# The fourth group's P of each two-layer step transposed by DMA, with a refitted planner and a new order of work

## The chip, the cores and the metric

One core of a Trainium2 chip runs the kernel. The metric is the time of one execution on the device in microseconds, the median of several runs. Beside it stands a profile of one execution, with every instruction's start and end.

The engines go by the profile's names: PE (TensorE: matmuls; PEld is its weight load), DVE (VectorE), ACT (ScalarE), POOL (GpSimd) and SP (SyncE, whose queue issues most of the DMAs). Each engine works through its own instructions in order and waits on semaphores for the others.

## The reference

Two layers, each of attention with a recurrent memory and of a gated feed-forward network, run over x of 2048 rows by 576:

```python
for s in range(n_seg):                      # 64 segments of 32 rows
    h = concatenate([mem, xs], axis=1)      # 8 rows of memory + 32 rows
    q, k, v = (einsum('btd,dhe->bhte', h, W) for W in (Wq, Wk, Wv))   # 32 heads of 128
    scores = where(mask, einsum('bhqe,bhke->bhqk', q, k) * scale, -1e9)
    o = einsum('bhqk,bhke->bhqe', softmax(scores), v)
    o = einsum('bhte,hed->btd', o, Wo)
    mem = o[:, :M, :]                       # the next segment's memory
    outs.append(o[:, M:, :])

x = x + A(layernorm(x), ...); x = x + B(layernorm(x), ...)            # layer 0
x = x + A(layernorm(x), ...); x = x + B(layernorm(x), ...)            # layer 1
# B: silu(x @ w1) * (x @ w3) @ w2, with 4608 hidden columns
```

A segment can't begin before the one ahead of it has given its memory. Both layers use the same weights.

## The kernel before, in words

**Steps.** Attention goes in 72 steps of one segment. Layer 1 runs 8 steps (`LAG`) behind layer 0, so 56 of the steps (8 to 63) work on a segment of each layer at once: 80 columns (2 x 40 rows) instead of 40. The other 16 have one layer. The weights of the attention stay in SBUF; those of the feed-forward network are streamed from HBM again for each 128 rows, into two buffers (W13) for w1 and w3 and two (W2C) for w2.

**Inside a step.** The 32 heads go in four groups of 8. A group takes these nodes, with the letter that each has in the written-out order of PE: Q and q (projections of q and k, 64-row remainder in q, two each per group), S (scores), then on DVE and ACT the softmax (`sm_add`, `sm_max`, `sm_exp`, `sm_sum`, and `sm_pb`, which writes P into the tile PB), then a transpose of P from PB into PTS, then P (P times V), a copy of its result, and O and o (times Wo). V comes from V, v, X, x or G, g. When the fourth o is done, the memory's columns are copied into HT, on which the next step's Q waits. The feed-forward network fills PE beside this: F and f (up), W and w (down), and p, n, a, b are small transposes around the layernorms.

**The transpose of P.** With `g < DMA_GROUPS` in a step with two layers, one DMA on SP's queue does it (`ptd`, L1027): it reads 112 partitions of PB and writes PTS. Otherwise it is the letter T: 8 matmuls with the identity (`ptr`, L1034) into two banks of PSUM, and two copies to PTS on ACT or DVE (`pt_ev`, L1044). PB has one buffer, PTS has two. With `DMA_GROUPS = 3` the fourth group of each such step, and all groups of steps with one layer, use T.

**The planner.** `make_nodes` (L232) makes the nodes with their durations in us, dependences and buffers. `plan` (L77) lays them out in planned time: PE takes its nodes in the order of the string `ORDER` (L222, made of `FIRST`, eleven times `FOUR`, and `LAST`; one `FOUR` is four steps with 18 pairs of the feed-forward network). Each other engine takes the node that can start first in planned time; a copy marked `AD` goes to ACT or DVE, whichever is free first. `LATS` (L33) are planned delays from one engine to the next, `SWITCH` what PE is charged for a new tiling mode; a node marked `full/col` takes the mode of its neighbours, and in `col` each of its matmuls is issued as two halves. `TRD, TRL` (L36) are the planned time of a transpose on SP's queue and its delay after that. The plan decides only the order in each engine's stream and which engine does a copy. When an instruction really starts, semaphores decide.

**SP's queue** holds, in the plan's order, the weight loads (`load_w13` L703, four DMAs a pair; `load_w2` L713, one) and the transposes. A DMA at its head that waits holds up all behind it.

Of the kernel before, what the change touches and what calls it, by code (L numbers as in the profile page):

```python
# [9 lines left out]
ACT = mybir.ActivationFunctionType  # L10
# [20 lines left out]

SWITCH = 0.098
LATS = {"PE": 0.205, "ACT": 0.165, "DVE": 0.14, "POOL": 0.04}  # L33
NOW = 1.0e18
DMA_GROUPS = 3
TRD, TRL = 0.6, 4.2  # L36
POOLS = {"bank": 8, "qkt": 4, "sme": 2, "pb": 1, "pts": 2, "ot": 4,
         "xr": 3, "xn": 2, "w13": 2, "w2": 2, "htt": 4}

# [37 lines left out]
def plan(nodes, pools, letters):  # L77


    for n in nodes:  # L80
        for d in n.deps:
            d.outs.append(n)
    kinds = {}
    for n in nodes:
        if n.eng == "PE":
            kinds.setdefault(KINDS[n.name], []).append(n)
    its = {k: iter(v) for k, v in kinds.items()}
    seq = [next(its[c]) for c in letters]
    assert len(seq) == sum(len(v) for v in kinds.values())
    free = {k: [0.0] * c for k, c in pools.items()}  # L90
    t_eng = {e: 0.0 for e in ("PE", "ACT", "DVE", "POOL", "DMA", "SWD")}
    ready = {e: [] for e in t_eng}
    both = []
    mode, run = [], []
    order = []

    def settle():
        for x in run:
            x.mode = mode[0]
        run.clear()  # L100
    at = 0

    def push(n):
        if n.eng != "PE":
            (both if n.eng == "AD" else ready[n.eng]).append(n)

    def est(e, n):
        t = max(t_eng[e], n.ready)
        need = {}
        for s in n.acq:  # L110
            if s.i is None:
                need[s.pool] = need.get(s.pool, 0) + 1
        for p, c in need.items():
            t = max(t, sorted(free[p])[c - 1])
        return t

    for n in nodes:
        if n.left == 0:
            push(n)
    while len(order) < len(nodes):  # L120
        best = None
        for e in t_eng:
            if e == "PE":
                cands = seq[at:at + 1] if at < len(seq) and seq[at].left == 0 else []
            else:
                cands = ready[e] + (both if e in ("ACT", "DVE") else [])
            if not cands:
                continue
            ests = [(est(e, n), n) for n in cands]
            t = min(x for x, _ in ests)  # L130
            if t >= NOW:
                continue
            if best is None or t < best[0]:
                best = (t, e, ests)
        if best is None:
            raise RuntimeError(f"the plan is stuck at {at}: {seq[at].name}")
        t, e, ests = best
        st, n = min((x for x in ests if x[0] <= t + 1e-9), key=lambda x: x[1].prio)
        dur = n.dur
        if isinstance(dur, tuple):  # L140
            dur = dur[0] if e == "ACT" else dur[1]
        if e == "PE":
            at += 1
            if not any(m in mode for m in n.mode):
                dur += SWITCH
                settle()
                mode = n.mode
            mode = [m for m in mode if m in n.mode]
            run.append(n)
        elif n.eng == "AD":  # L150
            both.remove(n)
        else:
            ready[e].remove(n)
        n.start, n.end, n.by = st, st + dur, e
        t_eng[e] = n.end
        for s in n.acq:
            if s.i is not None:
                continue
            f = free[s.pool]
            s.i = min((i for i in range(len(f)) if f[i] <= st + 1e-9), key=lambda i: f[i])  # L160
            f[s.i] = NOW
        late = LATS.get(e, 0.135) if n.lat is None else n.lat
        for s in n.rel:
            s.users -= 1
            s.end = max(s.end, n.end + late)
            if s.users == 0:
                free[s.pool][s.i] = s.end
        for m in n.outs:
            m.ready = max(m.ready, n.end + (0.0 if m.eng == e == "PE" else late))
            m.left -= 1  # L170
            if m.left == 0:
                push(m)
        order.append(n)
    settle()
    return order
# [20 lines left out]
def ewh(*ns):  # L196
# [2 lines left out]


FIRST = (
    "maqQQqqQSqQSTQqQqqTQqSQSvVxXPTOPTOPPooOOooQqqqqQQSQQSqVvQTqqSQqQPTSOPXToOTPxoPOOooaQQqqqqQSQQSqVvQTqQqSQqPSTPOOT"
    "PTOPoooOoQQqqqqQSQvVSQTQqqqQSqQTPSXPOTOPToxoPOOooQqqqpqQQSvVnQQqfqFSTQFSPQQqqfOTSFfPWTOPfFTOPFOfooooWQqqqQQSFqff"
    "VvQFQQSqqWSQqfqTQPFTOSFTPfXxPOWTOPFOffooooFQWQQqqqQSFqqfvVaSQTFfqfQFPSWTQQqqfOSFPFTOPWTOPfoooOoFfqqQQWSQQvqqVfSF"
    "QqqQTWqqSPQTQOoPSbOTXPxxTOPooOoXpQQqqQSnqqqfQQqSFQfvqVSFQFfPQqPFSfWOOFPffFTOPWOooooFfqqQQQSFfqqWQQSQQqqqfFGSgqgQ"
    "PGWOfoPFFSgfgGGPOTOPFOoooWqQfqQQSWFqqQQSfVvqqfQPFfFSaqqQQPWOSFofOFPWTOPffFOoooWqqQQSQQbqqQqgSqGQQPSqGQgqOSPGGggO"
    "PTOPoooOoQqqppQQSVqqqQnnQvSFfqqQQQSFqffPFOPowSWFffFOPwTOPWOoooFfqqqQQQQSffqFFGWwSFqgfqQQQPWQSwFqqffFGSgggGPGPOTO"
    "POOoooWowFqqfqQQQQqfSFSQQQqqqwWSVvffqFFPQWwSFffOPFOTwWfPFPOOooooWqqQQqqaSQQqqQQSbwgqGqSQQPGgGSgPOOoGPgTOPooOo"
)
FOUR = (  # L210
    "QppQqqVSqqvQQnnQSFqfqqQQSFqffFQwPWPSFffFOOPwTWPOOooooFfqqfQQFQQqqSWwFSGfqgqQQQPQqqfWSwFSGFfgggGPGPOOTFPOOooooWwF"
    "qffqQQQQqqSWFSVqfqvQQwFQqqffFSPQwFPWSffOOFPwTOPWOooooFqqfQQqqaSQQWSQQqqqqQQbSwGSgggGPGPOgGPOTOPoooOo"
)
LAST = (
    "QqqppQQSVqqqQQnSnvQQqqFPSqffFQOoSwWPFffFPOTOPWOoooFfqqqQQQQqSwSFFqqffQQQgqgGSGPFPqQWSwfggGGPOOTwWPOOooooFfqqqQQF"
    "QSFfqfVvQQWQqqSwFSPFqqffQQOSwFoPWffFPOTOPwOoooWFqfqqQQqWSQQwSFqfqfFQQWvvSVVqqQPQOSbwPXPOTOPooxOooQQppVqqqQSvqqQQ"
    "nnSQQqqfFSqfTFPQTOPSFwTFffTPOPOWOooooFqfqqQQVvqQSQFWwTSQqfqfFQQqqQSwPWSTFFTPffOOTPWPOOoowoFoFffvxXVqqQQWSwFqqfqQ"
    "QTQSQQfqqqFSPQWTwSFFTPffOTPOPOOWoooowFvfqqVQQwSQWQqqfqQSFFTfqQPTSWQPqqQTSOPOObwTxoooPXOoQQpqqqQSQVvqqnQSFfqQFTQS"
    "qqfTPQFfOSwPTFPOOTFPffoooOowvVqqQQQSQqqfqQSFqqqQQQSTwPTFFPSffXxOTOPwTFPOOffooooFQQqqqqQSQQSQfqqVvTSFQwQqqTFPSPfT"
    "OFPfwTOPOOooooFfqQQqqqQQSvQSQqqqVSTQqfQfPTSFPOTwFPOTOoPofOoopwfFFnfFFwfffFFwffwFFFffFwFwfffFFFwffFFwffFFwfffFFww"  # L220
)
ORDER = FIRST + FOUR * 11 + LAST  # L222

# [1 line left out]
class Opt:  # L225

    qk, qkt, sc, tr, pv, wo, wog, vm = 0.0079, -0.0342, 0.0268, 0.1447, 0.0406, 0.2653, 0.0725, 0.1407
# [4 lines left out]
def make_nodes(em, nseg, pools, o=Opt, dma_bw=230e3, load_bw=400e3):  # L232
# [4 lines left out]
    def node(*a, **k):  # L237
        n = Node(*a, **k)
        nodes.append(n)
        return n  # L240
# [117 lines left out]
    def step(t):  # L358
        ls = layers_of(t)
        nl = 2 if both(t) else 1  # L360
        c80 = 40 * nl
        e = role(t)
# [13 lines left out]
        for g in range(NG):  # L376
            qs, qe = [], []
            for u in (2 * g, 2 * g + 1):
# [4 lines left out]
                          prio=pq, mode="full", acq=[q] + b, name="QK")  # L383
                n = node("PE", 4 * mm80, em.qk_tail(t, u, b), deps=hx + hm + ([ld_h[u // 4]] if t == 0 else []), prio=pq + o.qkt, mode="row",
                         acq=[q] + b, name="QKt")
                rd += [m_, n]
                me[f"QK{u}"], me[f"QKt{u}"] = m_, n
                for r in (0, 1):
                    qe.append(node("AD", ew(256, 64) if nl == 2 else ew(160), em.qk_ev(t, u, r, q, b[r]), deps=[m_, n], prio=t + o.ustep * u,
                                   rel=[b[r]], name="QKe"))  # L390
                qs.append(q)
            s = banks(1)[0]
            sme = Slot("sme")
            pf = t + o.gstep * g
# [3 lines left out]
            c = node("ACT", 0.094 + 320 / 1200, em.sm_exp(t, g, sme), deps=[m_], prio=pf, name="exp")  # L398
            pb = Slot("pb")
            if g == 0 and t:  # L400
                zero = [node("POOL", 0.95, em.pb_zero(pb), deps=last_pt, prio=pf, acq=[pb], name="pbz")]
            else:
                zero = []
            d = node("DVE", 0.623 if nl == 2 else 0.606, em.sm_sum(t, g, sme), deps=[c], prio=pf, name="sum")
            w = (1.074 if e else 1.143) if nl == 2 else 0.466
            pbs = node("DVE", w, em.sm_pb(t, g, sme, pb), deps=[d] + zero, prio=pf, acq=[pb], rel=[sme], name="pb", lat=0.125 if nl == 2 else 0.225)
            pts = Slot("pts")
            if nl == 2 and g < DMA_GROUPS:
                pe_ = [node("DMA", TRD, em.ptd(t, g, pb, pts), deps=[pbs], prio=pf, acq=[pts], rel=[pb], name="TRD", lat=TRL)]
                last_pt[:] = pe_  # L410
            else:
                bt = banks(nl)
                tr = node("PE", 8 * (0.0258 if nl == 1 else 0.0358), em.ptr(t, g, pb, bt), deps=[pbs], prio=pf + o.tr, mode="full/col", acq=[pts] + bt, rel=[pb], name="TR")
                pe_ = [node("AD", ew(320), em.pt_ev(t, g, i, b, pts), deps=[tr], prio=pf, rel=[b], name="PTe") for i, b in enumerate(bt)]
                last_pt[:] = [tr]
            if paired(t):
# [6 lines left out]
                      prio=pf + o.pv, mode="full/col", acq=b + [ot], rel=[pts], name="PV")  # L423
# [933 lines left out]
```

## Time and profile before

| | before |
|---|---|
| median of 3 timed runs | 2689.06 us (2685.54 to 2690.9) |
| the profiled execution's own time | 2686.17 us |
| its span, first to last instruction | 2684.2 us |
| granted TensorE clock, mean | 0.993 |
| PE matmuls | 58657 records, busy 2593.0 us |
| DVE, ACT busy | 2086.2 us, 1260.1 us |
| transposes by DMA | 168 |
| weight loads of the feed-forward network, W13 | 612 of 256 KB and 612 of 32 KB, landing 3.7 and 3.5 us after issue |

How to read the profile's rows: a group of instructions has its line, engine, operation, the tiles it writes and reads (`out<-in`) and its count, then busy time and mean ns of one, then how long the engine sat idle before it and who ended that. A line is that of a helper here: all matmuls have L603, all of ACT L606, all of DVE L609, plain DMAs of SP L612. In the timeline the first column is the start, the second how long the row lasts, both in us; a row can merge several instructions.

### The profile page before, as it was taken

Reading aid. Unit: us, or ns where it says so; the run is one execution under the profiler, and the core shown is the slowest. Engines: PE = TensorE matmul, PEld = TensorE weight load, DVE = VectorE, ACT = ScalarE, POOL = GpSimd, SP = SyncE. Lnnn points to the kernel's source line nnn. Section 1 sums busy time; section 2 is a strip of 40 time slices with the busy share of each in tenths; the row PEclk is TensorE's granted clock in tenths of the full one; section 3 lists DMA queues with packets and bytes.
Section 4 is the critical chain, followed back from the end, with each engine's and each line's share of the span. In section 5 each row is a group of like instructions: output and inputs, shape, how many; then the busy total and the mean of one; then the engine's idle time right before and its main releaser. Section 6 shows DMA issues by size and latency. Waiting matters only on the chain.

```text
span 2684.2 us, 132015 instructions
## 1 busy us (share of the span) xinstructions
PE 2593.0 (97%) x58657; PEld 2234.0 (83%) x58700; DVE 2086.2 (78%) x5352; ACT 1260.1 (47%) x3649; POOL 130.1 (5%) x182
## 2 busy tenths in 40 slices
PE   5999999999999999999999999999999999999998
PEld 4788888788888888888888888888888888888887
DVE  4887787787788778778877877887887787787876
ACT  2655444444445354444535444453544445454453
POOL 1000000000000000000000000000000000000000
PEclk8999999999999999999999999999999999999999
DMA  9065635564453546446444544544464453445357
GB/s 318 4 186 132 162 99 146 112 146 125 117 140 99 139 118 149 126 120 144 100 128 116 149 129 115 146 98 131 115 149 126 124 144 96 118 124 149 110 162 259
DMA packets 634059, 360.30 MB, mean 134 GB/s; under 512 B 181928, under 2 KB 623664, under 8 KB 632848
## 3 DMA queue, kind: packets, MB, share of 16 engines
q1 hardware_dynamic: 629952, 343.99, 48.0%
q8 instruction: 459, 7.52, 1.2%
q0 software_dynamic: 3024, 6.93, 0.9%
q10 hardware_dynamic: 512, 0.94, 0.2%
q14 instruction: 112, 0.92, 0.1%
HBM read 308.49 MB, written 2.36 MB: 116 GB/s over the span
## 4 chain that ended last, share of the span: by engine, by line
PE 82%; DVE 6%; DMA 6%; ACT 3%; issue 2%; SPq 1%; ACTq 0%; POOL 0%; DVEq 0%; POOLq 0%
PE bank L603 82%; DMA W<-in_B_w_dram 3%; DVE V L609 1%; DVE STAT L609 1%; DMA W2C<-in_B_w_dram 1%; ACT V L606 1%; DVE SME L609 1%; SPq L612 1%; DVE HTT L609 1%; DVE XR L609 1%; DVE PB L609 1%; DMA WV<-in_A_Wv_dram 0%; DMA PTS<-PB 0%; ACT YTS L606 0%; ACT SME L606 0%
## 5 line engine op out<-in xcount | busy, mean ns | idle before, releaser
L603 PEld LDWEIGHTS <-W 128*128 128x128 bf16 (+2 forms) x32160 | 1263.1, 100 | 159.0 <-issue 69.8
L603 PE MATMUL bank<-HT,W 128*128 128x80 bf16 (+3 forms) x23040 | 798.6, 197 | 18.6 <-ACT HT L606 8.0
L603 PE MATMUL bank<-XTB,W 128*64 128x256 bf16 (+5 forms) x9120 | 668.5, 263 | 22.1 <-DMA W<-in_B_w_dram 18.9
L606 ACT ACTIVATE QKT<-bank 128x256 bf16<-128x256 f32 (+4 forms) x1546 | 356.7, 312 | 296.0 <-PE bank L603 237.3
L603 PE MATMUL bank<-OT,WO 128*128 128x80 bf16 (+2 forms) x11520 | 400.7, 198 | 5.0 <-ACT V L606 3.2
L603 PEld LDWEIGHTS <-WO 128*128 128x128 bf16 (+1 forms) x11520 | 375.6, 102 | 20.6 <-issue 11.5
L603 PE MATMUL bank<-WV,HT 128*32 128x512 bf16 (+4 forms) x3535 | 360.5, 384 | 9.2 <-issue 6.0
L606 ACT ACTIVATE V<-bank 32x512 bf16<-32x512 f32 (+1 forms) x551 | 317.9, 587 | 101.2 <-PE bank L603 91.6
L606 ACT ACTIVATE HTT<-bank 128x512 bf16<-128x512 f32 (+1 forms) x324 | 176.2, 550 | 356.6 <-PE bank L603 355.9
L603 PE MATMUL bank<-W2C,HTT 128*64 128x288 bf16 (+1 forms) x3176 | 320.8, 286 | 3.7 <-DMA W2C<-in_B_w_dram 2.3
L609 DVE TENSOR_REDUCE STAT<-SME 104x8 f32<-104x320 f32 (+1 forms) x576 | 275.3, 478 | 14.3 <-ACT SME L606 7.3
L609 DVE TENSOR_TENSOR PB<-SME,STAT 40x128 bf16<-40x128 f32 (+4 forms) x912 | 275.3, 336 | 11.5 <-DMA PTS<-PB 2.0
L609 DVE SCALAR_TENSOR_TENSOR HTT<-HTT,bank 128x512 bf16<-128x512 bf16 (+1 forms) x324 | 201.5, 622 | 99.3 <-ACT HTT L606 96.5
L603 PEld LDWEIGHTS <-HT 128*32 128x32 bf16 (+4 forms) x3576 | 153.7, 99 | 136.0 <-issue 27.3
L603 PEld LDWEIGHTS <-HTT 128*64 128x64 bf16 (+1 forms) x3240 | 229.1, 105 | 39.6 <-issue 6.5
L609 DVE SCALAR_TENSOR_TENSOR XR<-bank,XR 128x288 f32<-128x288 f32 x576 | 244.3, 449 | 12.8 <-PE bank L603 8.8
L606 ACT ACTIVATE SME<-SME 104x320 f32<-104x320 f32 (+1 forms) x288 | 135.7, 471 | 238.3 <-DVE SME L609 236.8
L609 DVE CAST V<-bank 64x512 bf16<-64x512 f32 (+1 forms) x313 | 213.6, 683 | 22.3 <-PE bank L603 15.1
L609 DVE TENSOR_TENSOR HTT<-HTT,bank 128x512 bf16<-128x512 bf16 (+1 forms) x324 | 203.6, 629 | 29.2 <-PE bank L603 0.5
L606 ACT ACTIVATE OT<-bank 128x320 bf16<-128x320 f32 (+1 forms) x381 | 143.5, 403 | 161.8 <-PE bank L603 158.9
L609 DVE CAST QKT<-bank 128x128 bf16<-128x128 f32 (+2 forms) x502 | 137.0, 315 | 83.0 <-PE bank L603 81.5
L609 DVE TENSOR_TENSOR SME<-bank,maskb 104x320 f32<-104x320 f32 (+1 forms) x288 | 139.0, 483 | 32.7 <-PE bank L603 27.4
(59 smaller groups left out, 1450.9 us busy)
## 6 DMA issues: line engine op xcount, KB each, us to landing
W<-in_B_w_dram SPq DMA_DIRECT2D x612, 256.0 KB, 3.7
W2C<-in_B_w_dram SPq DMA_DIRECT2D x306, 288.0 KB, 3.3
W<-in_B_w_dram SPq DMA_DIRECT2D x612, 32.0 KB, 3.5
W<-in_B_w_dram SPq DMA_DIRECT2D x8, 1024.0 KB, 11.9
W<-in_A_Wq_dram SPq DMA_DIRECT2D x9, 512.0 KB, 9.1
WO<-in_A_Wo_dram SPq DMA_DIRECT2D x4, 1152.0 KB, 16.8
XR<-in_A_x_dram POOLq DMA_DIRECT2D x16, 288.0 KB, 3.5
WV<-in_B_w_dram SPq DMA_DIRECT2D x4, 1152.0 KB, 10.3
```

What stands on the lines that cost most here:

```text
L603: self.ch("PE", self.nc.tensor.matmul(out, lhsT=lhsT, rhs=rhs, start=start, stop=stop, skip_group_check=True, **k))
L606: self.ch("ACT", self.nc.scalar.activation(*a, **k))
L609: self.ch("DVE", getattr(self.nc.vector, fn_)(*a, **k))
L612: self.ch("SP", self.nc.sync.dma_start(out=out, in_=in_))
```

## The change

- `DMA_GROUPS` goes from 3 to 4: in the 56 steps with two layers, the fourth group's P is also transposed by a DMA of SP's queue. `ptr` and `pt_ev` stay for the steps with one layer.
- The planner's durations: `TRD, TRL` change, a table `MORE` adds to the durations of some nodes by engine, and `sum` and `TR` have delays of their own.
- `FIRST`, `FOUR` and `LAST` are new strings. `FOUR` has the same letters, less its four T; `FIRST` has 8 and `LAST` 4 T fewer.

```diff
+MORE = {"ACT": {"VMe": 0.13, "VXe": 0.13, "VGe": 0.13, "Yodd": 0.145, "PTe": 0.03, "Fwr": 0.1, "QKe": 0.02, "exp": 0.03},
+        "DVE": {"VMe": 0.2, "VXe": 0.2, "VGe": 0.2, "mul": 0.07, "sum": 0.05, "add": 0.03, "POSTa": 0.12, "Fnorm": 0.13, "maxsub": 0.02},
+        "PE": {"SC": 0.05, "WOt": 0.03, "VG": 0.03, "FFt": 0.01, "TR": 0.01, "QK": 0.007}}
-DMA_GROUPS = 3
-TRD, TRL = 0.6, 4.2
+DMA_GROUPS = 4
+TRD, TRL = 1.24, 1.9
...
+        dur += MORE.get(e, {}).get(n.name, 0.0)
...
 FOUR = (
-    "QppQqqVSqqvQQnnQSFqfqqQQSFqffFQwPWPSFffFOOPwTWPOOooooFfqqfQQFQQqqSWwFSGfqgqQQQPQqqfWSwFSGFfgggGPGPOOTFPOOooooWwF"
-    "qffqQQQQqqSWFSVqfqvQQwFQqqffFSPQwFPWSffOOFPwTOPWOooooFqqfQQqqaSQQWSQQqqqqQQbSwGSgggGPGPOgGPOTOPoooOo"
+    "QqqqppQvVSQQnnQFfqqFSfqqQQFfqQSwPWPSFffOOWPFwFPOOooooFffqqQQwQQqqgSWGSFqqfQQQPQSWFqfqfFSwGgggGPGOPOPOOwoooFWoFff"
+    "qqQQQQqqSFSqqfQQwWvVSQQFfqqfFSPWPOOwFffPFOWPwOooooFqqfQQqqaSQQWqSQQqqqqQQSbwGSggGPGPggGPOOOPoooOo"
 )
...
-            d = node("DVE", 0.623 if nl == 2 else 0.606, em.sm_sum(t, g, sme), deps=[c], prio=pf, name="sum")
+            d = node("DVE", 0.623 if nl == 2 else 0.606, em.sm_sum(t, g, sme), deps=[c], prio=pf, name="sum", lat=0.14 if nl == 2 else 0.22)
...
-                tr = node("PE", ..., name="TR")
+                tr = node("PE", ..., name="TR", lat=0.265)
```

`plan` uses a node's `lat` in place of the delay in `LATS`. The branch that the first line of the change decides:

```python
            if nl == 2 and g < DMA_GROUPS:
                pe_ = [node("DMA", TRD, em.ptd(t, g, pb, pts), deps=[pbs], prio=pf, acq=[pts], rel=[pb], name="TRD", lat=TRL)]
```

In `pcols` (L1060) the columns of PTS that P reads follow from the same condition.

More of the change, by code (lines that the diff above doesn't have):

```diff
@@ L201 @@
 FIRST = (
[L202 to L206, printed above, removed]
@@ L207 @@
-    "PTOPoooOoQqqppQQSVqqqQnnQvSFfqqQQQSFqffPFOPowSWFffFOPwTOPWOoooFfqqqQQQQSffqFFGWwSFqgfqQQQPWQSwFqqffFGSgggGPGPOTO"
-    "POOoooWowFqqfqQQQQqfSFSQQQqqqwWSVvffqFFPQWwSFffOPFOTwWfPFPOOooooWqqQQqqaSQQqqQQSbwgqGqSQQPGgGSgPOOoGPgTOPooOo"
+    "maQQQqqqqQSQQTSqQQqSTqqSvVXxPPTOPOTOooPoOoQqqqqQQSQQSqvVQqQSqTQqXPSTOPTOaooPxTOPoOoQqqQQSQqqvVqSQqqQQqSTQPSTOPOT"
+    "PTOPoooOoQqqqqQQSQvVSqqQQqqQQSTPTSXPOoTxPTOPOOoooQqqqpQQvVSqnQQqfSFQQqqqQSTFfTSPFOfPoTWPOFTOPfooOoFQQqqqfQSFfqqV"
+    "vQWSQQFqfqTQSFWqfPQOTFPSfXWoTxfOPTFPOOoooFfqqQQFSQfqVvqqQWSQTFfqfFQQPSWTQfqqOPSFTOPFWTOPooffOooFQQqqqqQSQWVvSFfq"
@@ L209 @@
+    "QQTqWqqSQPTQaOSPbOTXPxooTOPxoOoXpqqQQqqQSQqvnQSfFQqVSfqFQfFPqQfFSPWfFPOoOOoofFPWOoFQQqfqfFSQqqqqQQQSWGSqqgQQFfgP"
+    "GSWPGFfggfFGPOOWPOOooooFfqqQQQfSFqqQvFSWVfqqQQfFSWqQQqfPPSFOOFoPWOffFPaooOoWQqqqqQQSbQQSGgqqqQQgSPGqQOSPGOgGPgoO"
+    "PooOoQqqqppQQQvSqqVnnSQFqqfQQFPSqffQFPOSoWwFFPffOOWPwOoooFqffqQQFwQQqqfSWGFSFqgqfQQQPQSWFqfqgGSwggGPGOPOOPWOFooo"
+    "oFffqqQQQQqqawSSFfqqqQQQWvSwVffqFQFPPWSwFfOOPFWwffFPOOooooWQQqqqQSqqqQQQSbwGSgqqgQQPGSggGPGOPOOPoooOo"
 )
 FOUR = (
-    "QppQqqVSqqvQQnnQSFqfqqQQSFqffFQwPWPSFffFOOPwTWPOOooooFfqqfQQFQQqqSWwFSGfqgqQQQPQqqfWSwFSGFfgggGPGPOOTFPOOooooWwF"
@@ L212 @@
-    "qffqQQQQqqSWFSVqfqvQQwFQqqffFSPQwFPWSffOOFPwTOPWOooooFqqfQQqqaSQQWSQQqqqqQQbSwGSgggGPGPOgGPOTOPoooOo"
+    "QqqqppQvVSQQnnQFfqqFSfqqQQFfqQSwPWPSFffOOWPFwFPOOooooFffqqQQwQQqqgSWGSFqqfQQQPQSWFqfqfFSwGgggGPGOPOPOOwoooFWoFff"
+    "qqQQQQqqSFSqqfQQwWvVSQQFfqqfFSPWPOOwFffPFOWPwOooooFqqfQQqqaSQQWqSQQqqqQQSbwGSggGPGPggGPOOOPoooOo"
 )
 LAST = (
-    "QqqppQQSVqqqQQnSnvQQqqFPSqffFQOoSwWPFffFPOTOPWOoooFfqqqQQQQqSwSFFqqffQQQgqgGSGPFPqQWSwfggGGPOOTwWPOOooooFfqqqQQF"
-    "QSFfqfVvQQWQqqSwFSPFqqffQQOSwFoPWffFPOTOPwOoooWFqfqqQQqWSQQwSFqfqfFQQWvvSVVqqQPQOSbwPXPOTOPooxOooQQppVqqqQSvqqQQ"
@@ L217 @@
[L217 to L220, printed above, removed]
+    "QpqqqQpQSvqqQQnSVqQnQFPSffqqFQOPSFOwPooffOFPWOooFqfqqQQQQfqSWwGSgqFQFPQwQqqfGSFfqgQOPSWggGGPOFPOOoWowooFfqfqQQQQ"
@@ new lines @@
+    "qqSWFSfqqQQwVvFSFfqqfQQPWOPSwFoOoffFPwPOOoWoFfqqqQQQQSWwqfFSFfqqQQWvvVSVqqPQQOSbwXPxPOOPoooOoQQpqqpVvqqQSQQqSnnQ"
+    "QqqFTSffqFPTQOPSWFffTFPTOOPwOooooFfqqQQQSQQvqqqVwFWSfqfFqqQQQTSwWSFPTffOTPFOTPwPOOooooWFfqfqFQQQSQqqvxXVwWSFTFff"
+    "qqQQQwqqSQTPWPffSFOTFPwTOPOWOooooFvfqqVQQWSFQqfqQwSFfqqQQqTSqWQPTQOTSPPoOObwTxoPXOooQQqqvpSQQqqVSnqQFfqQFTSQfqPQ"
+    "qfTFSPOTwFPOOTFPffooOoowVqqqvQQQSQfqqFSQQqqqwQSTQPFTSOPXffOTFPTxOPwOooooFFqqffQQqqQSQQSqqVvqfQFTSQwPQqfTOSFPFTOf"
+    "PwTOPFOfooooQQqqqQSvqqQVSqQTQSPQQqqTOSPFwTFffPOTOPoooOopwfFnFfffFFwFwfffFFFwffFFwfffFFwFwfffFFFwffFFwfffFFww"
@@ L412, in step @@
                 bt = banks(nl)
-                tr = node("PE", 8 * (0.0258 if nl == 1 else 0.0358), em.ptr(t, g, pb, bt), deps=[pbs], prio=pf + o.tr, mode="full/col", acq=[pts] + bt, rel=[pb], name="TR")
+                tr = node("PE", 8 * (0.0258 if nl == 1 else 0.0358), em.ptr(t, g, pb, bt), deps=[pbs], prio=pf + o.tr, mode="full/col", acq=[pts] + bt, rel=[pb], name="TR", lat=0.265)
                 pe_ = [node("AD", ew(320), em.pt_ev(t, g, i, b, pts), deps=[tr], prio=pf, rel=[b], name="PTe") for i, b in enumerate(bt)]
```

## The prediction

> **What bounds the kernel now.** I read the page first, then the stretches, then TensorE's waits. The page says which engine is full:
>
> ```profile
> span 2684.2 us, 132015 instructions
> ...
> PE 2593.0 (97%) x58657; PEld 2234.0 (83%) x58700; DVE 2086.2 (78%) x5352; ACT 1260.1 (47%) x3649; POOL 130.1 (5%) x182
> ...
> PE 82%; DVE 6%; DMA 6%; ACT 3%; issue 2%; SPq 1%; ACTq 0%; POOL 0%; DVEq 0%; POOLq 0%
> ```
>
> TensorE is busy for 97% of the span and carries 82% of the chain that ended last. The profiled execution took 2686.17 us, its span 2684.2; the median of the three timed runs is 2689.06 (2685.54 to 2690.9), 2.9 us above the profiled one. I add up against 2686.2 and add 2.9 at the end. The view by stretches separates the repeated middle from both ends (columns: length, then busy time of PE, PEld, DVE, ACT, POOL, then clock):
>
> ```profile
> 0.00:100.00 100.00, 68.87 (x1844) 54.10 (x1845) 59.14 (x153) 38.73 (x106) 8.83 (x21) 0.87 0.61 215
> 1301.00:1457.00 156.00, 153.01 (x3303) 132.81 (x3305) 122.67 (x313) 73.04 (x214) 7.41 (x10) 1.00 0.50 127
> 2237.00:2684.00 447.00, 429.42 (x10271) 366.10 (x10272) 341.58 (x868) 208.48 (x582) 19.11 (x24) 1.00 0.51 147
> ```
>
> One round of the written-out order FOUR (four steps) takes 156 us; TensorE idles 3.0 us of it. Of its 91 us idle in all, 31 lie in the first 100 us, where the weights arrive, and 18 in the last 447. So about 60 us of idle time is all that a better order could win; the rest must come out of work. The waits of TensorE name the idle time (columns: us, times, longest):
>
> ```profile
> PE bank L603 <- DMA W<-in_B_w_dram: 18.9, 21, 1.9
> PE bank L603 <- issue: 14.1, 51, 2.1
> ...
> PE bank L603 <- DMA PTS<-PB: 0.5, 2, 0.4
> ```
>
> FFN weights that come late are the largest; the 168 transposes by DMA hold TensorE up for 0.5 us together. The old order leaves them more room than they use.
>
> **What goes: TensorE's transposes.** The order of the instructions of the changed kernel has no 80-column matmul from PB left: 448 go (8 in each of 56 steps with two layers), with 448 weight loads, and 112 copies from PSUM to PTS.
>
> ```profile
> L603 PE MATMUL bank<-ident,PB 104*128 104x80 bf16 x448 | 25.8, 201 | 0.8 <-DVE PB L609 0.8
> L606 ACT ACTIVATE PTS<-bank 128x320 bf16<-128x320 f32 x130 | 55.1, 436 | 59.8 <-PE bank L603 54.7 <-DMA W<-in_B_w_dram 2.0 <-DVE HTT L609 1.1
> L609 DVE CAST PTS<-bank 128x320 bf16<-128x320 f32 x46 | 22.5, 490 | 21.8 <-PE bank L603 20.1
> ```
>
> The 25.8 us are a union of overlapping records, with the last matmul's tail in each group. What a group costs is the distance to the next one's start; the timeline of PE around the fourth group of a step shows it:
>
> ```profile
> 1305.19 0.45 PE L603 MATMUL bank<-PTS,V 128*128 128x80 bf16 x8
> 1305.48 1.31 PE L603 MATMUL bank<-OT,WO 128*128 128x80 bf16 x32
> 1306.62 0.45 PE L603 MATMUL bank<-ident,PB 104*128 104x80 bf16 x8
> 1306.91 1.31 PE L603 MATMUL bank<-OT,WO 128*128 128x80 bf16 x32
> 1308.06 0.45 PE L603 MATMUL bank<-PTS,V 128*128 128x80 bf16 x8
> 1308.44 0.76 PE L603 MATMUL bank<-OT,WO 128*64 128x80 bf16 x25
> ```
>
> From 1306.62 to 1306.91 are 0.29 us; 56 x 0.29 = **-16.2 us**. The bound on the other side is the whole 25.8. The copies run on ACT and DVE beside TensorE's work (DVE 78%, ACT 47% busy): I cost them at nothing. If DVE were the bound, they would bring 46 x 0.49 at most, and a few more, since the new order also moves other copies from DVE to ACT (DVE has 5013 rows before, 4819 after).
>
> **What the new order adds on TensorE.** Counting by the plans, TensorE changes its tiling mode 63 times a round, not 60, and 1198 times in all, not 1155: 43 more. The price: O after P in the same mode starts after 0.29 us (1305.19 to 1305.48), and o, in another mode, after 0.38 (1308.06 to 1308.44), 0.09 more. 43 x 0.09 = **+3.9 us**; the least is nothing, where the wait for a copy hides it. Of the P matmuls, 256 become 512 half-wide ones:
>
> ```profile
> L603 PE MATMUL bank<-PTS,V 128*128 128x80 bf16 x1616 | 91.7, 201 | 0.4 <-DVE HTT L609 0.3
> L603 PE MATMUL bank<-PTS,V 128*64 128x80 bf16 x352 | 10.7, 202 | 0.4 <-DMA PTS<-PB 0.4
> ```
>
> 91.7/1616 is 57 ns, two halves are 2 x 30.4 = 61 ns: 256 x 4 ns = **+1 us**.
>
> **What it adds on SP's queue.** 56 more transposes, so 224:
>
> ```profile
> L1028 SPq DMA_TRANSPOSE PTS<-PB x168: 1222/1240/2626, 244.2 to 2391.5; - x168
> ...
> DMA to landing us min/median/max: 2.6/2.8/5.5
> ```
>
> ```profile
> SPq L612 <- PE bank L603: 907.8, 607, 77.5
> SPq L1028 <- DVE PB L609: 673.9, 138, 21.5
> ```
>
> 56 x 1.24 = 69 us of SP's time; SP waits over 1580 us in these two rows, and that covers it. But the queue is in order: behind a transpose that waits for PB stand weight loads of the FFN, and behind those the F of TensorE. What a late weight load costs is seen in one place of the timelines of PE and SP:
>
> ```profile
> 1321.95 1.91 PE L603 MATMUL bank<-XTB,W 128*64 128x256 bf16 x31
> 1323.95 0.38 PE L603 MATMUL bank<-XTB,W 64*128 64x256 bf16 x4
> ...
> 1325.05 2.27 SPq L612 DMA_DIRECT2D W<-in_B_w_dram  x4
> ...
> 1330.33 0.93 PE L603 MATMUL bank<-XTB,W 64*128 64x256 bf16 x7 [0.62 <-DMA W<-in_B_w_dram]
> ```
>
> The buffer is free at 1324.33; its next contents are used at 1330.33, 6.0 us later, 0.62 of them idle. So two F that share a buffer want 6.0 us of other work between them. The old order is shortest at F S P Q w (2.0 + 0.3 + 0.3 + 1.2 + 0.9, 4.7 us) and at F with two Q (about 5); the new one at q q F S f q q Q Q (about 5.4), its others are near 5.6 to 6. I take **-2 us** of the 18.9; the bounds are -10 (half of them gone) and +19 (twice as many).
>
> **The new wait.** P of a step's fourth group now hangs on a landing. PB has one buffer, so the third group must have landed before DVE may write the fourth. The last step of a round, with S and the transpose of its third group, and DVE before the PB of its fourth:
>
> ```profile
> 1293.33 0.40 PE L603 MATMUL bank<-QKT 128*64 128x40 bf16 x15
> 1300.07 1.22 SPq L1028 DMA_TRANSPOSE PTS<-PB  x1
> ...
> 1302.98 0.67 DVE L609 CAST V<-bank 64x512 bf16<-64x512 f32 x1
> 1303.58 1.05 DVE L609 TENSOR_TENSOR PB<-SME,STAT 40x320 bf16<-40x320 f32 x3
> ```
>
> S of the third group starts at 1293.33, its transpose is issued at 1300.07 and has landed by 1302.87 (median 2.8). The fourth PB takes 1.05, its transpose 2.8 more: 1302.87 + 0.03 + 1.05 + 0.06 + 2.8 = 1306.8, 13.5 us after S of the third. The new order puts S b w G S gg G P G P gg G P OOO before that P. With b 0.38, w 0.94, G 1.51 to 1.75, P 0.29 and O 1.15, from starts to starts of these rows:
>
> ```profile
> 1292.95 0.45 PE L603 MATMUL bank<-ident,XN 128*128 128x128 bf16 x5
> ...
> 1293.60 1.15 PE L603 MATMUL bank<-W2C,HTT 128*64 128x288 bf16 x15
> 1294.54 1.93 PE L603 MATMUL bank<-WV,HT 128*64 128x512 bf16 x16
> 1296.29 0.42 PE L603 MATMUL bank<-QKT 128*40 128x40 bf16 x16
> 1296.65 0.82 PE L603 MATMUL bank<-WV,HT 64*128 64x512 bf16 x6
> 1297.63 1.67 PE L603 MATMUL bank<-WV,HT 128*128 128x512 bf16 x7 [0.16 <-issue]
> 1299.14 0.45 PE L603 MATMUL bank<-PTS,V 128*128 128x80 bf16 x8
> ```
>
> they are 14.1 us: 0.6 of slack. Counted the same way, the first step of a round has about 0.8, the second about 1, the third 4. And in the trace PB began at 1303.58, 0.7 after that landing, since DVE was copying V. Two of four steps thus stand at about nothing. Between 0 and 0.7 us a step, I take 0.15 on the 28 tight ones (DVE is less busy in the new order): **+4 us**; the upper end is 28 x 0.7 = 20, and 39 where the third group's P is late too.
>
> The Trainium skill ("DMA: Bandwidth & Descriptors", section "Queues, rings and completion order") says that each DMA engine consumes one queue's descriptors in ring order. The 5.5 in the landing row agrees with it; what it would make of the fourth transposes is rival four.
>
> **Sum.** -16.2 + 3.9 + 1.0 - 2 + 4 = -9.3: 2686.2 becomes 2676.9, and on the median's footing 2679.8. I say **2679**. About 0.2% (5.4 us) is what a measurement of this kernel can tell from no change.
>
> **Rivals.**
> 1. *The new order also removes waits.* For: the old one gave the transposes more room than they need (0.5 us waited for 168). Against: the weights' two buffers are the same. Half of the 60 us idle gone is 30, of which the sum has 2: 2679 - 28 = 2651.
> 2. *The saving is covered.* TensorE's 16 us turn into waits elsewhere, as for the weights at the upper bound's half (+10): 2689, no change.
> 3. *The single PB decides: slower.* Four landings in a row, each with DVE's 1.05 between, end after P's place. It decides once the fourth P is late by over 13/28 = 0.5 us in the tight steps. For: the 0.7 above. Against: 0.6 to 0.8 of slack, 42 copies fewer on DVE for PTS alone. With 0.7 to 1.4 a tight step: -13 + 20 to 39, 2696 to 2715, say 2704.
> 4. *Landings behind loads: slower.* A transpose right behind a weight load lands at 5.5, not 2.8: 2.7 less 0.7 of slack, once a round in the first step and once in the third, 28 x 2 = 56 less 13: 2732 if always, 2704 if half of the time. Against: the median of 2.8, with loads ahead of many of the 168.
> 5. *The change isn't what it says.* The instruction order shows the 224 transposes; left is that the freed time was never on the path: 2689.
>
> **Chances.** Forecast 0.42 (its own range 2670 to 2687), rival 1 0.20, rival 2 0.14, rival 3 0.15, rival 4 0.07, rival 5 0.02. The forecast's range lies below 2683.7 in nine parts of ten: faster 0.38 + 0.20 = 0.58, same 0.04 + 0.14 + 0.02 = 0.20, slower 0.22. The range goes from 2651 (half of rival 1 is below) to 2706 (half of rivals 3 and 4 is above).
>
> **What would show it.** Right: a round of 155 us or a little more; TensorE's busy time down by 10 to 20; 224 transposes at 1.24; waits of TensorE for PTS of a few us; weight waits near 17. Wrong: TensorE waiting for PTS by over 15 us (rivals 3, 4; in 4 the landings' median rises), the row of late weights doubled (2), or idle time in a round under 2 us (1).

## The result, and the profile after

| | before | after |
|---|---|---|
| median | 2687.3 us (4 runs, 2685.09 to 2690.9) | 2657.02 us (4 runs, 2651.48 to 2660.02) |
| ratio to before, 95% interval | | 0.9884, 0.9863 to 0.9904 |
| the profiled execution | 2686.17 us | 2657.81 us |

The change is 30 us (1.2%) faster. The prediction had the sign, but it forecast 8 us against the median of 2687.3. The time lies 22 us from the forecast (2679) and 6 us from rival 1 (2651), "the new order also removes waits". The range (2651 to 2706) holds it because it was drawn wide enough to take in half of that rival.

The page of the changed kernel, the rows that answer to the first ones of before:

```profile
span 2656.0 us, 131716 instructions
...
PE 2579.5 (97%) x58546; PEld 2209.3 (83%) x58546; DVE 2011.5 (76%) x5145; ACT 1265.5 (48%) x3744; POOL 128.8 (5%) x182
...
PE 85%; DMA 8%; DVE 3%; issue 1%; SPq 1%; ACT 1%; POOL 0%; ACTq 0%; DVEq 0%; POOLq 0%
```

The span is 28.2 us shorter: TensorE's busy time fell by 13.5 (2593.0 to 2579.5), its idle time by 14.7 (91.2 to 76.5). The forecast had -11.3 for the first and +2 for the second. So the busy part came out as worked out, and the idle part is the surprise. Ten rounds of `FOUR` in the view by stretches, from one clearing of PB on POOL to the same one ten rounds later (before first, then after):

```profile
685.49:2245.02 1559.53, 1532.74 (x33045) 1330.67 (x33073) 1230.37 (x3131) 735.91 (x2141) 74.07 (x100) 1.00 0.49 127
```

```profile
676.50:2218.45 1541.95, 1523.40 (x33039) 1312.30 (x33036) 1184.51 (x3000) 731.26 (x2190) 73.93 (x101) 1.00 0.54 134
```

A round went from 156.0 to 154.2 us in the mean. The ten are 17.6 us shorter, 9.3 of it busy time and 8.2 idle time; the other 10.6 us of the span lie outside them, in the parts that `FIRST` and `LAST` order for the most part. TensorE's waits in the changed kernel (us, times, longest), and below them two of its weight-load queue, first before, then after:

```profile
PE bank L607 <- DMA PTS<-PB: 14.7, 21, 1.6
...
PE bank L607 <- issue: 10.1, 12, 2.4
...
PE bank L607 <- DMA W<-in_B_w_dram: 5.5, 8, 1.9
...
PE bank L607 <- ACT V L610: 1.7, 2, 1.5
```

```profile
PEld L603 <- DMA W<-in_B_w_dram: 26.7, 33, 2.2
```

```profile
PEld L607 <- DMA W<-in_B_w_dram: 9.6, 15, 2.1
```

The waits for PTS rose from 0.5 to 14.7 us, as the new wait should; those for FFN weights fell from 18.9 to 5.5 (26.7 to 9.6 in the rows of the weight loads), far more than the 2 us I gave them. Where, the timelines of PE show. In the kernel before they stood at two places of a round: 23 to 32 us after its start in most of the rounds, and some 117 us after it in a few (rounds from 1151.58, 1307.19, 1463.76):

```profile
1174.86 2.44 PE L603 MATMUL bank<-XTB,W 64*128 64x256 bf16 x20 [0.87 <-DMA W<-in_B_w_dram]
...
1424.12 0.60 PE L603 MATMUL bank<-XTB,W 64*128 64x256 bf16 x4 [0.76 <-DMA W<-in_B_w_dram]
...
1487.16 2.24 PE L603 MATMUL bank<-XTB,W 64*128 64x256 bf16 x19 [0.88 <-DMA W<-in_B_w_dram]
...
1580.73 0.59 PE L603 MATMUL bank<-XTB,W 64*128 64x256 bf16 x4 [1.12 <-DMA W<-in_B_w_dram]
```

In the changed kernel (rounds from 1139.10, 1292.58, 1446.12) one place is left, some 31 us after the start and in about half of the rounds, and the PTS waits come now here, now there:

```profile
1169.78 0.58 PE L607 MATMUL bank<-XTB,W 64*128 64x256 bf16 x4 [0.42 <-DMA W<-in_B_w_dram]
1200.29 0.46 PE L607 MATMUL bank<-PTS,V 128*128 128x80 bf16 x8 [0.41 <-DMA PTS<-PB]
...
1323.15 0.39 PE L607 MATMUL bank<-XTB,W 64*128 64x256 bf16 x3 [0.38 <-DMA W<-in_B_w_dram]
1414.28 0.45 PE L607 MATMUL bank<-PTS,V 128*128 128x80 bf16 x8 [0.78 <-DMA PTS<-PB]
```

The transposes themselves, in the view of the tile PTS:

```profile
L1032 SPq DMA_TRANSPOSE PTS<-PB x224: 1222/1238/2668, 244.5 to 2370.3; - x112
...
DMA to landing us min/median/max: 2.6/2.9/5.8
```

224 of them as counted, 1.24 us each on SP, and in the median they land as before (2.9 for 2.8 us). Most of the waits for PTS follow late ones among them. Two places, each with the transpose on SP and the P that waits for it:

```profile
981.70 1.22 SPq L1032 DMA_TRANSPOSE PTS<-PB  x1
986.41 0.45 PE L607 MATMUL bank<-PTS,V 128*128 128x80 bf16 x8 [1.23 <-DMA PTS<-PB]
```

```profile
1409.63 1.23 SPq L1032 DMA_TRANSPOSE PTS<-PB  x1
1414.28 0.45 PE L607 MATMUL bank<-PTS,V 128*128 128x80 bf16 x8 [0.78 <-DMA PTS<-PB]
```

From issue to P are 4.7 us in both, 1.8 more than the median landing.

### The profile page after: what moved, and what is told of

Read it like the earlier page. It is cut to its first block, busy times and chain, and to the rows that moved or that the text cites. A ratio compares the mean times of both kernels' runs of the same rounds, so it can differ in the third digit from the quotient of the medians.

```text
span 2656.0 us, 131716 instructions
## 1 busy us (share of the span) xinstructions
PE 2579.5 (97%) x58546; PEld 2209.3 (83%) x58546; DVE 2011.5 (76%) x5145; ACT 1265.5 (48%) x3744; POOL 128.8 (5%) x182
## 4 chain that ended last, share of the span: by engine, by line
PE 85%; DMA 8%; DVE 3%; issue 1%; SPq 1%; ACT 1%; POOL 0%; ACTq 0%; DVEq 0%; POOLq 0%
PE bank L607 85%; DMA PTS<-PB 5%; DMA W<-in_B_w_dram 2%; SPq L616 1%; DVE PB L613 1%; DMA W<-in_A_Wk_dram 1%; DMA W2C<-in_B_w_dram 1%; DVE STAT L613 0%; DVE SME L613 0%; DVE HTT L613 0%; DMA XN<-in_A_x_dram 0%; ACT V L610 0%; ACT HT L610 0%; DVE XR L613 0%; ACT SME L610 0%
## 5 line engine op out<-in xcount | busy, mean ns | idle before, releaser
L607 PE MATMUL bank<-HT,W 128*128 128x80 bf16 (+3 forms) x23040 | 791.4, 197 | 13.9 <-issue 7.2
L610 ACT ACTIVATE QKT<-bank 128x64 bf16<-128x64 f32 (+2 forms) x1645 | 377.4, 309 | 282.5 <-PE bank L607 270.8
L610 ACT ACTIVATE V<-bank 32x512 bf16<-32x512 f32 (+1 forms) x577 | 324.9, 584 | 161.5 <-PE bank L607 155.4
L607 PE MATMUL bank<-WV,HT 128*32 128x512 bf16 (+5 forms) x3592 | 366.7, 384 | 0.7 <-issue 0.7
L607 PEld LDWEIGHTS <-HT 128*32 128x32 bf16 (+5 forms) x3592 | 152.2, 99 | 145.8 <-issue 40.3
L610 ACT ACTIVATE OT<-bank 128x320 bf16<-128x320 f32 (+1 forms) x430 | 157.9, 403 | 229.4 <-PE bank L607 224.5
L613 DVE CAST V<-bank 64x512 bf16<-64x512 f32 (+1 forms) x287 | 196.1, 686 | 20.7 <-PE bank L607 14.8
L613 DVE CAST QKT<-bank 128x128 bf16<-128x128 f32 (+4 forms) x403 | 108.4, 316 | 100.0 <-PE bank L607 98.3
```

The source lines that it names most:

```text
L607: self.ch("PE", self.nc.tensor.matmul(out, lhsT=lhsT, rhs=rhs, start=start, stop=stop, skip_group_check=True, **k))
L610: self.ch("ACT", self.nc.scalar.activation(*a, **k))
L613: self.ch("DVE", getattr(self.nc.vector, fn_)(*a, **k))
```

## The experiments

The theories. **A**: the new strings for TensorE removed the waits. **B**: the refitted durations did, through the order of work on SP, ACT and DVE. **C**: the 56 transposes on TensorE cost more than 0.29 us each. All times are medians; ratios are to the kernel before, run beside it.

**e1, the refitted durations alone** (old strings, three groups):

```diff
-DMA_GROUPS = 4
+DMA_GROUPS = 3
-FIRST, FOUR, LAST = the new strings
+FIRST, FOUR, LAST = the old strings
```

> The old order of TensorE and three groups by DMA, with the new planned durations alone: they change only how SP, ACT and DVE order their work and which of the two does a copy. Theory A (the new strings for TensorE removed the waits): within 4 us of before, 2683 to 2691, waits of TensorE for FFN weights near 18.9. Theory B (the refitted durations removed them): 10 to 15 us faster, 2672 to 2677, weight waits under 10. Theory C (the 56 transposes on TensorE cost more than 0.29 us each, because of their copies and banks): as A.

Measured: 2712.7 us, 1.0087 (1.0072 to 1.0102): 23 us slower than before. No theory had this. Its waits of TensorE:

```profile
PE bank L607 <- DVE PB L613: 13.9, 13, 2.5
...
PE bank L607 <- DMA W<-in_B_w_dram: 10.2, 16, 1.6
...
PE bank L607 <- DMA PTS<-PB: 5.6, 3, 4.6
```

The weights' wait fell, but TensorE now waits 13.9 us for DVE's PB (3.7 before) and 8.0 for V from DVE (0.9 before). The edit reorders only SP, ACT and DVE, so these waits come from there; which work went ahead of PB stays open. B as stated falls.

**e2, the fourth group by DMA alone** (old durations, old strings less the 56 letters T):

```diff
-DMA_GROUPS = 3
+DMA_GROUPS = 4
 the T of the 56 steps with two layers taken out of FIRST, FOUR, LAST
```

> The fourth group by DMA alone: old durations, old order less the 56 letters T of the steps with two layers. Theory A: 16 us less work and some 5 us of new waits for PTS, since the old order leaves no room for a fourth landing: 2672 to 2680, weight waits near 19. Theory B: the same, 2672 to 2680. Theory C: 25 us or more faster, 2655 to 2662.

Measured: 2798.3 us, 1.0408 (1.0387 to 1.0428), 109 us **slower**. A had the mechanism and not nearly the size; C in its strong form falls. A round, and TensorE's waits in it and in all:

```profile
1361.67:1526.81 165.14, 155.61 (x3281) 134.12 (x3281) 121.69 (x310) 71.63 (x209) 7.41 (x11) 0.98 0.53 125
```

```profile
1401.91 0.45 PE L603 MATMUL bank<-PTS,V 128*128 128x80 bf16 x8 [3.09 <-DMA PTS<-PB]
1447.10 0.46 PE L603 MATMUL bank<-PTS,V 128*128 128x80 bf16 x8 [1.27 <-DMA PTS<-PB]
...
1492.70 0.69 PE L603 MATMUL bank<-PTS,V 128*128 128x80 bf16 x8 [3.03 <-DMA PTS<-PB]
```

```profile
PE bank L603 <- DMA PTS<-PB: 90.8, 38, 4.8
```

The order without its T leaves the fourth P less room than a landing takes. That alone isn't all of it. SP and DVE ahead of the two waits of 3 us:

```profile
1392.91 5.21 SPq L612 DMA_DIRECT2D W<-in_B_w_dram  x8
1398.22 1.25 SPq L1028 DMA_TRANSPOSE PTS<-PB  x1
...
1483.37 6.54 SPq L612 DMA_DIRECT2D W<-in_B_w_dram  x8
1490.00 1.25 SPq L1028 DMA_TRANSPOSE PTS<-PB  x1
```

```profile
1394.53 1.12 DVE L609 TENSOR_TENSOR PB<-SME,STAT 40x128 bf16<-40x128 f32 x4
```

```profile
1485.79 1.13 DVE L609 TENSOR_TENSOR PB<-SME,STAT 40x128 bf16<-40x128 f32 x4
```

PB is written at 1395.65 and at 1486.92, and its transposes are issued 2.6 and 3.1 us later, because SP is still issuing weight loads that the plan put ahead of them. So at these two places it is SP's order, more than the single PB of rival 3, that makes P late. At the third (1447.10) the transpose goes out at once, at 1442.38, and P starts 4.7 us later.

**e3, the fourth group and the refitted durations on the old order:**

```diff
 the changed kernel, with
-FIRST, FOUR, LAST = the new strings
+FIRST, FOUR, LAST = the old strings less the 56 T
```

> The fourth group by DMA and the new durations, on the old order less its 56 T: the changed kernel without the new order. Theory A: 2670 to 2678, and the new order is worth the remaining 13 to 20 us. Theory B: 2655 to 2662, no more than the measurement's noise above the changed kernel. Theory C: 2655 to 2662, with no gain from the durations over the fourth group alone.

Measured: 2773.0 us, 1.0319 (1.0302 to 1.0336). Its wait for PTS is 65.3 us. None of the theories had it; the new strings are worth 116 us on this footing (2773.0 to 2657.0).

**e7, the 56 transposes on TensorE issued twice**, in the kernel before:

```diff
-            for j in range(GH):
+            for j in list(range(GH)) * (2 if nq == SW else 1):
```

> The kernel before with the 8 matmuls of each of the 56 transposes on TensorE issued twice (the second time over the same result). The step of 0.29 us a group: +16 us, 2703. If a group's matmuls hide in waits anyway: +0 to 5 us. If they cost their whole busy time of 25.8 us in the profile: +26, 2713.

Measured: 2701.8 us, 1.0049 (1.0036 to 1.0062): +12 us, 0.22 us a group (10 to 17 us by the interval). It is 0.29 or a little under. In the profile TensorE's busy time is 14.9 us longer (2607.9, 2593.0 before), 0.27 us a group. The matmuls thus cost no more than was taken. The copies and banks that C also names aren't doubled here; e4 bears on them.

**e4, the changed kernel with T back:**

```diff
-DMA_GROUPS = 4
+DMA_GROUPS = 3
-"...ffOOWPFwFP...GPGOPOP...FffPFOWP...GPggGPOOOP..."
+"...ffOOWPFwTFP...GPGOPTOP...FffPFOTWP...GPggGPOOTOP..."  (T one large letter ahead of each fourth P, in all 56 steps)
```

> The changed kernel with three groups by DMA again: the new strings and new durations, with a T put back one large letter ahead of P of the fourth group in each of the 56 steps. If the 56 transposes on TensorE cost what their doubling cost (+12 us), and the new order owes nothing to the fourth landing: 2669. If the new order is good only with the fourth group by DMA, because a T one letter ahead of its P waits for its copies and its two banks: 2680 and above. Theory C in its strong form (nothing but T mattered): 2687.

Measured: 2667.1 us, 0.9921 (0.9907 to 0.9936): as the expectation for T at the cost of its doubling has it. Its page and its waits:

```profile
PE 2597.5 (97%) x59010; PEld 2228.2 (84%) x59010; DVE 2028.0 (76%) x5179; ACT 1298.0 (49%) x3822; POOL 129.0 (5%) x182
```

```profile
PE bank L607 <- DMA W<-in_B_w_dram: 6.4, 7, 1.8
...
PE bank L607 <- DMA PTS<-PB: 5.8, 9, 1.5
```

So some 21 of the 30 us (17 to 25 by the interval) are there **without** the fourth group by DMA: they belong to the new strings with the durations that fit them. The fourth group adds about 10 (3 to 17 by the two intervals). The profiles say what each part is made of (one execution each, with granted clocks of 0.993, 0.994 and 0.995). From the kernel before to e4 (span 2664.4), TensorE's busy time rose by 4.5 and its idle time fell by 24.3 (91.2 to 66.9). From e4 to the changed kernel the busy time fell by 18.0, and the idle time rose by 9.6, of which the waits for PTS are 8.9 (5.8 to 14.7). The 56 transposes were worth 18 us of work, 0.32 a group, and the new wait took half of that back. TensorE's wait for ACT's copies to PTS is 1.4 us in both, so the copies that C names add nothing that this row shows.

**e5, the changed kernel with the old durations:**

```diff
-TRD, TRL = 1.24, 1.9
+TRD, TRL = 0.6, 4.2
 and without MORE, the delay of sum, and that of TR
```

> The changed kernel with the old planned durations (a transpose of 0.6 + 4.2 us, nothing from MORE): TensorE's order is the new one, SP, ACT and DVE are laid out by the old durations. If TensorE's order alone makes the gain: 2653 to 2665. If order and durations must fit each other, as refitting alone on the old order cost 23 us: 2680 or above, with new waits of TensorE for PB's writers and copies.

Measured: 2843.5 us, 1.0574 (1.0560 to 1.0588). TensorE's order is written out as in the changed kernel, and the run is 186 us slower than that. A falls too: the strings without their durations lose. That is shown with the fourth group by DMA only; new strings with old durations and T kept were not run.

```profile
PE bank L603 <- DMA PTS<-PB: 115.9, 64, 4.6
```

**e10 and e11, W13's loads cut to a quarter**, in the kernel before and in the changed one:

```diff
-                self.dma(W[:, 4 * kind:4 * kind + 4], wd[0:4 * P, fa:fa + 2 * P]...)
+                self.dma(W[:, 4 * kind:4 * kind + 1], wd[0:P, fa:fa + 2 * P]...)
+    nc.vector.memset(T.W13[:], 0.0)      # once, at the start
```

> The kernel before with W13's large loads cut to a quarter (only the first 128 of 512 rows of w1 and w3 are loaded; the rest of the buffer stays zero, so the output isn't the reference's), in the same number of DMAs. It takes away most of the wait of TensorE for FFN weights (18.9 us in the profile). If these waits are on the path in full: 14 to 19 us faster, 2669 to 2675. If they only give way to the next wait: 0 to 6 us faster.

> The same cut in the changed kernel (again only a quarter of w1 and w3 is loaded, so the output isn't the reference's), where TensorE waits 5.5 us for FFN weights. If the fall from 18.9 to 5.5 explains the part of the gain that the transposes' 12 us leave over: 3 to 6 us faster than the changed kernel, 2651 to 2655, so 10 to 14 us less than the same cut brings in the kernel before. If the weights had nothing to do with it: the same gain in both.

Measured: e10 2662.2 us, 0.9907 (0.9892 to 0.9922), 25 us faster than before. e11 2644.1 us, 0.9831 (0.9818 to 0.9844), against the changed kernel's 0.9884 some 14 us faster. The cut brings 11 us less in the changed kernel (3 to 18 by the intervals): about that much of the weights' cost its order had taken out already. Each cut brought more than expected and more than TensorE's row of waits (18.9 and 5.5 us). Their rows:

```profile
PE bank L603 <- DMA W<-in_B_w_dram: 7.1, 8, 2.8
```

```profile
PE bank L607 <- DMA PTS<-PB: 16.3, 20, 2.5
...
PE bank L607 <- DMA W<-in_B_w_dram: 1.8, 2, 1.1
```

The profiled execution of e10 is the longest of its five (2671.7 us), and its span is 14.4 us below that of before: the row of the weights fell by 11.8, and the one called "issue", in which no releaser shows, by 8.8 (14.1 to 5.3). So a part of what late weights cost stands in a row without their name. In e11 the waits for PTS stay (16.3), so they don't come from the bytes of W13's loads. The cut also takes three quarters of these bytes off the DMA engines, so its whole gain needn't be the wait alone.

**e12, e13, e14: the planner's delays raised to the trace's**; e12 and e13 also have new strings, two sequences of moves of single letters that made the plan shorter:

```diff
-TRD, TRL = 1.24, 1.9
+TRD, TRL = 1.24, 2.2
-... acq=[w13], lat=2.0, name="W13")]
+... acq=[w13], lat=2.7, name="W13")]
-... acq=[w2], lat=2.0, name="W2l"))
+... acq=[w2], lat=2.5, name="W2l"))
 e12, e13: FIRST, FOUR, LAST moved as said; e14: left
```

> The changed kernel with the planner's delays after a load and a transpose raised to what its trace shows (W13's loads 2.0 to 2.7, W2C's 2.0 to 2.5, a transpose 1.9 to 2.2), and the three strings changed by moving single letters up to five places wherever the plan came out shorter. If TensorE's remaining waits for weights (5.5 us) and for PTS (14.7) come from delays that the plan sets too short: 8 to 16 us faster than the changed kernel, 2641 to 2649, both waits down by half or more. If these waits are the scatter of the transfers, which no plan foresees: 2652 to 2660.

> The same delays, another sequence of moves of letters from the same start. It tells how much of the result hangs on one string. Expected as for the other: 2641 to 2649 if the delays matter, 2652 to 2660 if not, and the two within 6 us of each other.

> The changed kernel with the raised delays alone, its strings as they are. As the refit alone on the old order and the old durations on the new order both lost, a plan whose durations no longer fit its strings should lose here too: 2675 or above. If truer delays help by themselves: 2657 or below.

Measured: e12 2653.7 us, 0.9868 (0.9854 to 0.9882); e13 2660.1, 0.9891 (0.9877 to 0.9905); e14 2702.1, 1.0047 (1.0030 to 1.0065). e12's interval overlaps that of the changed kernel (0.9863 to 0.9904) and so does e13's: nothing gained that can be told. Waits of e12, then e14:

```profile
PE bank L607 <- DMA PTS<-PB: 8.4, 11, 1.9
...
PE bank L607 <- DMA W<-in_B_w_dram: 6.4, 7, 1.8
```

```profile
PE bank L607 <- DMA PTS<-PB: 43.4, 38, 4.6
```

The waits for PTS fell in both (14.7 to 8.4 in e12 and 9.9 in e13), those for weights didn't (5.5 to 6.4 and 5.7); what is left looks like the scatter of the landings, as in the two places above, more than like a wrong delay, which isn't shown. e14 is e1 and e5 once more: three delays changed by 0.3 to 0.7 us, strings kept, 45 us lost.

## Why the prediction was right in sign and small in size

1. *TensorE's transposes, -16.2*: right, in mechanism and in size. TensorE's busy time differs by 18.0 us between e4 and the changed kernel, and by 14.9 for the doubling in e7. (The counts of DVE's rows that the prediction gives, 5013 and 4819, are not the pages', 5352 and 5145; the difference is much the same, and the sum doesn't use it.)
2. *43 changes of mode and the halved P, +4.9*: borne out as a sum, though not measured apart: e4, with the new strings and T kept, is busy for 4.5 us more than before. With the first term they make -11.3, and TensorE's busy time fell by 13.5.
3. *Late weights, -2*: **this is the mis-sized term**. TensorE's row fell by 12.5 in e4 and by 13.4 in the changed kernel, and the two cuts put the difference at 11 us. I compared the shortest runs of letters (4.7 and 5 in the old order, 5.4 to 6 in the new) with 6.0, found both orders short of it, and took 2 us of a bound of 10. In the traces the waits stood at two places of the old round and at one of the new.
4. *The new wait, +4*: TensorE waits 14.7 us for PTS, of the sign and kind foreseen. The fourth group brought 8.9 of that, twice the term; 5.3 came with the new order and three groups. It didn't decide, because other waits fell more. Added up again from its own rows, the run of letters ahead of the fourth P is 14.3 to 15.2 us, not 14.1, so the slack was larger than 0.6. But it was counted against a landing of 2.8 us; at the two places shown, issue to P took 4.7. Rival 3, which had the single PB decide, is not what the changed kernel shows.
5. *Idle time as a whole*: the prediction bounded it (60 us outside the start) and gave rival 1 a chance of 0.20, by which half of it goes. The sum had no term for waits other than those for weights and PTS, and the prediction gave no reason for leaving the others out. The order took 24.3 us out (before to e4): besides the weights' 12.5, ACT's V went from 7.7 to 1.8, "issue" from 14.1 to 8.8 and DVE's YTS from 3.8 to 1.0. No run took these apart.
6. *Landings behind loads* (the ring order that the Trainium skill states in "DMA: Bandwidth & Descriptors", section "Queues, rings and completion order"): landings stayed at 2.9 us in the median and 5.8 at most with 56 more transposes, so rival 4's sign is absent. Late landings do cost TensorE waits, but e11's wait for PTS didn't fall with a quarter of W13's large loads; no run here shows that the loads ahead are what makes a landing late.

So the forecast had the part that it worked out, the work that leaves TensorE, and missed the larger one, the waits that the new order removes. That its range held the time is owed to the rival, not to the sum: the number inside the range is luck as far as the sum goes. Two of the signs that it set up agree with this: idle time in a round went from 2.7 to 1.9 us, under the 2 that stood for rival 1, and the wait for PTS came to 14.7 us, just under the 15 that stood for rivals 3 and 4.

Durations and order, two edits in the list of changes, act as one. e1, e5 and e14 each change one side only and lose 23, 186 and 45 us. The planner's durations don't touch TensorE's order; they decide in which order DVE writes PB among its other work, where a transpose stands among SP's loads, and which engine copies what. The old strings and the new ones each did worse with durations other than those that they came with. The old strings less their T, which came with neither, did 25 us better with the new durations (2798.3 to 2773.0).

## What to carry to other kernels

- Where a plan fixes the order of every engine, a change of its durations is a change of every stream but the written-out one: judge durations and order together, and don't add up the effects of one without the other (durations and strings together -21 us with three groups, the durations alone +23).
- Removing an operation from the full engine was worth about its start-to-start distance (16.2 us worked out, 15 to 18 measured); what takes its place decides the sign (the same DMA: -10 us with the new strings and durations, +109 with the old ones).
- Don't price a change of order by one row of waits. Take the load away, or put the old operation back, and read busy and idle time apart: the weights' row had 18.9 us, their cut brought 25 in the median and 14 in the profiled execution, and a part of that stood under "issue".

## What the hardware showed that I had not expected

Waiting costs more than its own time. e2 issues 448 matmuls fewer than the kernel before and its TensorE is busy for 2612.7 us, not 2593.0; the granted clock over the run is lower. e2, then e5, in the view of the cores:

```profile
core 0: 2792.9 us, clock 0.981
```

```profile
core 0: 2840.6 us, clock 0.974
```

Before it was 0.993, after 0.995. In e2's round above, whose longest wait is 3.09 us, the granted clock is 0.98; over the ten rounds of the kernels before and after, whose waits stay mostly under a microsecond, it is 1.00. The view by stretches shows it around that wait, which ends at 1401.91 (the last three columns are the clock, the DMA engines' share and GB/s):

```profile
1398.82:1401.91 3.09, 0.00 (x1) 0.00 (x1) 0.46 (x1) 0.00 (x0) 0.00 (x0) 1.00 1.01 184
1403.27:1406.68 3.41, 3.41 (x71) 3.29 (x69) 0.00 (x0) 0.00 (x0) 0.00 (x0) 0.50 0.03 6
```

The granted clock is 0.50 over a stretch of 3.41 us that begins 1.4 us after the wait. The Trainium skill ("TensorE: Matmul & The Clock Gate", "Part 1: The HAM clock gate") has the clock fall to half after an idle window of about 3.4 us; the trace agrees in kind: here it follows a visible wait of 3.09 us. Of e2's 109 us, 89 are idle time (180.2 us, 91.2 before) and 20 the longer busy time, with the 448 matmuls gone.
